# A two-layer state-space and long-convolution kernel: the list scheduler's ranks come from a table of wanted times, and A1's norm, W, G0 and the tables are computed and placed in another way

## The chip, the cores and the metric

The kernel runs on one NeuronCore of a Trainium2 chip. The metric is the device time of one execution in microseconds (us). The core has a matrix engine (PE, with its weight loads as PEld), a vector engine (DVE), a scalar engine (ACT), GpSimd (POOL) and a queue engine (SP) that issues most DMAs. Each engine executes its own instructions in the order in which the program gives them; engines wait for each other by semaphores.

## The reference

Two layer types are applied in turn, A, B, A, B, each added to a residual stream x of 2048 tokens by 640 features (bfloat16 in and out):

```python
def A(x):                      # x is already normalized, see below
    Lam_bar = exp(dt * Lam)                              # complex, 640 states
    B_bar = ((Lam_bar - 1) / Lam)[:, None] * Bmat        # 640 x 640, complex
    Bu = einsum("bld,pd->blp", x, B_bar)
    h[t] = Lam_bar * h[t-1] + Bu[:, t]                   # over 2048 tokens
    return 2 * einsum("blp,dp->bld", h, Cmat).real + x * Dskip

def B(q, k, v):                # q is the normalized x; k and v are inputs
    kv = v * (4-tap causal shift filter of k along the tokens)
    y = irfft(rfft(kv padded to 4096) * rfft(ssm_k padded))[:2048]
    return q * (y + kv * ssm_D)

x = x + A(layernorm(x)); x = x + B(layernorm(x), k, v)
x = x + A(layernorm(x)); x = x + B(layernorm(x), k, v)
```

The long convolution does not depend on x. The kernel computes it once and uses it in both B layers.

## The kernel before, in words

The program is a list of several hundred tasks, each with one engine (or a choice of ACT and DVE), dependencies, buffers and an estimate of its duration. `Sched.run` (from L121) walks through a simulated time: whenever an engine is free, it takes, among the tasks whose dependencies and buffers are there, the one with the highest rank, and the instructions are written out in the order in which tasks began. In the kernel before, a task's rank is the longest path from it to the end plus a fixed bias per part of the program:

```python
            t.path = t.est + tail + max((s.path for s in t.succ), default=0.0)
            t.rank = t.path + t.bias
```

The order of the instructions on each engine is fixed by this when the program is built.

**Phase 1, before the tokens.** The parts are: the sine tables (names `yt_*`; `FA` and `HA` are small tables that stage A and the last inverse stage need, computed on POOL with one sine on ACT each). The kv products in five blocks of 128 features: k and v are loaded transposed by SP (L907, L911), the shift filter is eight matmuls with diagonal weights for each half (L922), DVE multiplies by v (L928, the "gate"), and SP stores the block to DRAM (L932). Layer A's matrices: B is loaded and transposed by PE (L435, and with the discretization L450/451) and copied to `BT`. W0 and W1, which are C scaled by a factor per state, are made on PE as products of C (loaded transposed by SP in ten pieces, L405) with diagonal matrices `fd` that POOL builds (L343): 80 matmuls (L418/419) and 20 evacuations. G0, the direct part, is five groups (one per k) of matmuls of B with W0 (L500, L503). The rotation tables `tab` and `rtab` come from a chain of DVE, POOL and ACT instructions (L460 to L486).

Then five Y passes `yq0` to `yq4`, one per 128 features, compute the long convolution: loads of the filter and of kv, stage A (L964), stage B (L986 to L991) for the filter and for kv, the pointwise product of spectra on DVE (six instructions over 2176 elements, L1043 to L1048, called `pw`), the inverse stage IB on PE (L1067/1068), a DMA transpose by SP (`tt`, L1080), the last stage IA (L1096), and a store to DRAM (L1106). Every PE stage goes through one of four PSUM buffers, which ACT (L240) or DVE (L242) evacuates.

**Phase 2, over the tokens.** Each layer works on four chunks of 512 tokens, c0 to c3. A chunk of layer A has: layer-norm statistics (for A1 on ACT: 16 sums over the four chunks, L1236, and 16 squares, L529; for the other layers the sums come with the previous step, and ACT squares), the normalization (ACT L548 or DVE L550), a DMA transpose (`tu`, L575), 100 matmuls with BT (`bp`, L589/592), the rotation of states on DVE (`ri`, L611 to L613), two scans on DVE (L627), the rotation back (`ro`, L650 to L652), 110 or 118 matmuls with W and G (`cp`, L678), and the evacuation with the residual (`xe`, ACT L686/688 or DVE L690). A chunk of layer B is the norm, the normalization (`u`), a product with y and an addition on DVE (L714 with L716 in B1, L714 with L718 in B2, "a pair" here), and in B2 the store of the result.

## Time and profile before

| | |
|---|---|
| median of 3 runs | 424.05 us (423.93 to 424.08) |
| the profiled execution | 424.33 us |
| its span | 422.6 us |
| mean granted PE clock | 0.953 |
| PE busy | 350.3 us, 83% |
| DVE busy | 319.0 us, 75% |
| ACT busy | 251.5 us, 60% |
| POOL busy | 43.5 us, 10% |

The span goes from the first to the last instruction of one profiled execution; the rest of its time lies outside it. A row of slices divides the span into 40 equal parts of 10.6 us and shows each engine's busy share in tenths, 9 for 90% or more; PEclk is the clock granted to PE, in tenths. A row of the list of waits names an engine and a line, what it waited for, the sum in us, how often, and the longest. A row of the chain or of a timeline has the start and the duration in us, then engine and line; what stands in square brackets is the idle time ahead of it and what ended that. A row of costs has the number of instructions, then busy us and the mean of one in ns, then the idle time ahead. PE's matmuls are pipelined: one that is shown as 0.22 us long starts 0.055 us after the one before.

### The profile page before, as it was taken

How to read it: one execution, taken by the hardware profiler on the slowest of the kernel's cores; microseconds unless marked ns; L12 is line 12 of the kernel's file. 1: busy time of each engine (PE TensorE's matmuls, PEld its weight loads, DVE VectorE, ACT ScalarE, POOL GpSimd, SP SyncE). 2: the span in 40 equal slices, each digit the busy share in tenths (PEclk: the TensorE clock that was granted, in tenths of full speed). 3: DMA queues.
4: the chain of work that ended last, by engine and by line, in shares of the span. 5: the costliest groups of instructions: out<-in, count | busy, mean ns of one | idle time of the engine just before them, and what ended most of it. 6: DMA issues, size and time to landing. Idle time of an engine off the chain costs nothing.

```text
span 422.6 us, 8138 instructions
## 1 busy us (share of the span) xinstructions
PE 350.3 (83%) x3412; PEld 259.5 (61%) x3412; DVE 319.0 (75%) x430; ACT 251.5 (60%) x432; POOL 43.5 (10%) x81
## 2 busy tenths in 40 slices
PE   0596889589978898998699999999999926999920
PEld 0556758345667897897575955676887514755510
DVE  2789996301498789799999569726999995897396
ACT  1665977553899998997322764596855103402970
POOL 8727510420000000000000000000000000000000
PEclk9998999989999999999699999999999986999975
DMA  5919995944357972947721221541500300003023
GB/s 107 298 53 207 199 188 138 217 64 174 72 121 134 203 151 55 213 123 144 199 57 62 64 64 32 156 84 43 124 2 2 62 0 2 32 2 95 0 95 153
DMA packets 112542, 44.24 MB, mean 105 GB/s; under 512 B 105461, under 2 KB 106746, under 8 KB 112506
## 3 DMA queue, kind: packets, MB, share of 16 engines
q1 hardware_dynamic: 109130, 41.57, 43.8%
q10 hardware_dynamic: 3376, 2.16, 1.7%
q8 instruction: 26, 0.43, 0.4%
q14 instruction: 10, 0.08, 0.1%
HBM read 17.38 MB, written 7.86 MB: 60 GB/s over the span
## 4 chain that ended last, share of the span: by engine, by line
PE 39%; DVE 36%; ACT 10%; DMA 7%; issue 5%; POOL 2%; POOLq 0%; SPq 0%; DVEq 0%; ACTq 0%
PE ps L678 13%; DVE b L627 5%; PE ps L589 5%; PE ps L592 5%; ACT junk L529 5%; DMA b<-b 5%; DVE b L242 4%; PE ps L500 3%; DVE b L716 3%; DVE b L714 3%; PE ps L922 2%; PE ps L1067 2%; PE ps L1068 2%; DVE b L718 2%; PE ps L964 2%
## 5 line engine op out<-in xcount | busy, mean ns | idle before, releaser
L240 ACT ACTIVATE b<-ps 128x1024 bf16<-128x1024 f32 (+3 forms) x106 | 90.9, 909 | 27.5 <-PE ps L592 16.1
L678 PEld LDWEIGHTS <-b 128*128 128x128 bf16 x880 | 67.7, 98 | 48.9 <-issue 0.6
L678 PE MATMUL ps<-W,b 128*128 128x128 bf16 (+1 forms) x640 | 95.8, 299 | 0.0
L589 PE MATMUL ps<-b,BT 128*128 128x256 bf16 x400 | 59.4, 281 | 15.2 <-DVE b L690 11.6
L242 DVE CAST b<-ps 128x1024 bf16<-128x1024 f32 (+2 forms) x43 | 48.7, 1162 | 15.1 <-PE ps L1068 6.2
L592 PE MATMUL ps<-b,BT 128*128 128x256 bf16 x400 | 58.5, 278 | 0.0
L529 ACT ACTIVATE junk<-b,nmean 128x640 bf16<-128x640 f32 (+1 forms) x64 | 52.9, 827 | 1.6
L589 PEld LDWEIGHTS <-BT 128*128 128x128 bf16 x400 | 40.0, 101 | 20.9 <-issue 11.8
L627 DVE TENSOR_TENSOR_SCAN b<-rtab,b 128x1290 bf16<-128x1290 f32 x16 | 44.6, 2832 | 0.2
L592 PEld LDWEIGHTS <-BT 128*128 128x128 bf16 x400 | 40.1, 100 | 5.4
L548 ACT ACTIVATE b<-b,nmr,rstd 128x640 bf16<-128x640 f32 (+1 forms) x38 | 32.6, 911 | 15.7 <-DVE nmr L541 15.7
L524 ACT ACTIVATE nmean<-sums 128x4 f32<-128x4 f32 (+1 forms) x19 | 3.9, 203 | 59.3 <-DVE b L690 45.9
L986 PE MATMUL ps<-b,b 128*128 128x128 bf16 x170 | 35.1, 219 | 0.9 <-ACT b L240 0.6
L989 PE MATMUL ps<-b,b 128*128 128x128 bf16 x170 | 35.2, 219 | 0.0
L991 PE MATMUL ps<-b,b 128*128 128x128 bf16 x150 | 32.8, 219 | 0.0
L988 PE MATMUL ps<-b,b 128*128 128x128 bf16 x150 | 32.8, 219 | 0.0
L678 PE MATMUL ps<-G,b 128*128 128x512 bf16 (+1 forms) x160 | 27.0, 299 | 0.5 <-DVE b L690 0.5
L928 DVE TENSOR_TENSOR b<-ps,b 128x1024 bf16<-128x1024 f32 x10 | 12.1, 1222 | 18.6 <-PE ps L922 17.5
L964 PE MATMUL ps<-FA,b 128*128 128x256 bf16 x160 | 22.0, 283 | 3.1 <-ACT b L240 1.6
L539 DVE RECIPROCAL rstd<-std 128x4 f32<-128x4 f32 (+1 forms) x19 | 3.2, 168 | 24.4 <-ACT std L534 24.4
L964 PEld LDWEIGHTS <-b 128*128 128x128 bf16 x160 | 15.7, 101 | 7.2 <-issue 4.4
L1067 PE MATMUL ps<-b,b 128*128 128x128 bf16 x160 | 18.8, 219 | 1.5 <-DVE b L928 0.8
(204 smaller groups left out, 626.2 us busy)
## 6 DMA issues: line engine op xcount, KB each, us to landing
b<-in_A_x_dram SPq DMA_DIRECT2D x8, 640.0 KB, 4.2
b<-ysd SPq DMA_DIRECT2D x8, 640.0 KB, 4.4
kvd<-b SPq DMA_DIRECT2D x5, 512.0 KB
b<-kvd SPq DMA_DIRECT2D x5, 512.0 KB, 5.1
ysd<-b SPq DMA_DIRECT2D x5, 512.0 KB, 4.0
out_dram<-b SPq DMA_DIRECT2D x8, 320.0 KB, 2.3
b<-in_B_ssm_k_dram SPq DMA_DIRECT2D x4, 512.0 KB
b<-in_A_B_re_dram ACTq DMA_DIRECT2D x1, 800.0 KB
```

The source lines that it names most:

```text
L240: nc.scalar.activation(out, in_, ACT.Copy)
L242: nc.vector.tensor_copy(out, in_)
L529: nc.scalar.activation(small.junk, src(q), ACT.Square, bias=st["nmean"][:, i:i + 1], scale=1.0, accum_out=st["ssq"][:, i:i + 1])
L589: nc.tensor.matmul(pb[:, jj, c2, :], lhsT=aw["BT1"][:, c2, j, k, :], rhs=uT[:, k, 0:2, :].rearrange("p t i -> p (t i)"), start=(k == 0), s ...
L592: nc.tensor.matmul(pb[:, jj, c2, :], lhsT=aw["BT0"][:, c2, k, j * P:(j + 1) * P], rhs=uT[:, k, 2:4, :].rearrange("p t i -> p (t i)"), star ...
L627: nc.vector.tensor_tensor_scan(gv, rt, gv, 0.0, ALU.mult, ALU.add)
L678: nc.tensor.matmul(pc[:, o0:o1], lhsT=lh, rhs=rh, start=(n == 0), stop=(n == len(ops) - 1))
L964: nc.tensor.matmul(pa[:, o4, :], lhsT=s_x.get()[:, 4 * g + o4, :], rhs=T["FA"][:], start=True, stop=True)
L986: nc.tensor.matmul(ps[:, g, 0, :], lhsT=T["Cf"].get()[:, q, :], rhs=are, start=True, stop=single)
L988: nc.tensor.matmul(ps[:, g, 0, :], lhsT=T["Sf"].get()[:, q, :], rhs=A[:, 2 * q + 1, :], start=False, stop=True)
L989: nc.tensor.matmul(ps[:, g, 1, :], lhsT=T["NSf"].get()[:, q, :], rhs=are, start=True, stop=single)
L991: nc.tensor.matmul(ps[:, g, 1, :], lhsT=T["Cf"].get()[:, q, :], rhs=A[:, 2 * q + 1, :], start=False, stop=True)
```

## The change

1. **Order.** A table `WHEN` gives a number to each group of tasks (the name up to a colon; some 270 groups), and the rank becomes minus this number plus a thousandth of the path. Some estimates of durations and latencies are other numbers too. So the order of the instructions is another one on all engines.
2. **W.** W0 and W1 are made by ACT (one C part scaled by a factor per partition into a float buffer) and DVE (`scalar_tensor_tensor`: the other part times its factor plus that buffer), 20 instructions each over 640 elements. The 80 matmuls, the POOL diagonals and the 20 evacuations go. C is loaded for W0 and again for W1: 20 DMA transposes of 128 x 640 instead of ten.
3. **B and G0.** B is loaded in ten pieces by ACT's queue directly into the tiles in which G0 and `tab` will stand later, so two large buffers are free. G0's matmuls need W0 (not W1) and stand ahead of the tables; the tables wait for all of G0's matmuls.
4. **Norm of A1.** `bn_stats` on DVE (two instructions of 320 columns and one `bn_aggr` per 128 tokens) in place of ACT's sums and squares.
5. **FA and HA.** POOL makes only the index ramps; the arithmetic is on DVE, the sine on ACT.
6. The small parameter vectors are loaded by ACT's queue instead of SP's.

The diff, cut to its core:

```diff
+WHEN = {
+    "yt_io0": -271.6, "yt_ph0": 326, "yt_sin0": -120, "yt_neg0": -228.7, "yt_io6": 435.5, "yt_ph6": 22.8, "yt_sin6": -279.2, "yt_neg6": -141, "yt_io12":
...
+}
-            t.rank = t.path + t.bias
+            t.rank = t.path + t.bias if WHEN is None else 0.001 * t.path - WHEN.get(t.name.partition(":")[0], 0)
...
-            nc.scalar.dma_start(out=s_B[i].get(), in_=src.rearrange("(j p) e -> p j e", p=P))
+            for k in range(NJ):
+                nc.scalar.dma_start(out=B[i][:, k], in_=src[:, k * P:(k + 1) * P].rearrange("(j p) e -> p j e", p=P))
...
-                    for d0, d1 in ((0, 512), (512, D)):
-                        nc.tensor.matmul(pw[:, d0:d1], lhsT=fd[:, 3 * w + c, :], rhs=wr[:, 0, d0:d1], start=True, stop=False)
-                        nc.tensor.matmul(pw[:, d0:d1], lhsT=fd[:, 3 * w + c + 1, :], rhs=wr[:, 1, d0:d1], start=False, stop=True)
...
+                def e_wc(_, w=w, c=c, j=j, s_wr=s_wr):
+                    nc.scalar.activation(s_wr.get()[1], s_wr.get()[0][:, 1, :], ACT.Copy, scale=st["F6"][:, w, c + 1, j:j + 1])
+                def e_wm(_, w=w, c=c, j=j, s_wr=s_wr):
+                    nc.vector.scalar_tensor_tensor(aw["W1" if w else "W0"][:, c, j, :], s_wr.get()[0][:, 0, :], st["F6"][:, w, c, j:j + 1], s_wr.get()[1],
+                                                   ALU.mult, ALU.add)
...
-        t_m = S.add(f"a_gm{k}", "pe", 10 * c_mm(512) + 11 * c_mm(P), [t_dd] + ws + T["tab"], e_gm, uses=[s_pg] + s_B)
+        t_m = S.add(f"a_gm{k}", "pe", 10 * c_mm(512) + 11 * c_mm(P), [t_dd] + w0s + bms, e_gm, uses=[s_pg])
...
-    t_t0 = S.add("a_t0", "dve", 5.7, [t_p4], e_t0)
+    t_t0 = S.add("a_t0", "dve", 8.3, gms, e_t0, uses=[s_tt])
...
+            for h in range(2):
+                nc.vector.bn_stats(bs[:, h, :], src(q)[:, h * (D // 2):(h + 1) * (D // 2)])
+            nc.vector.bn_aggr(st["mv"][:, q, :], bs[:])
...
-                nc.scalar.activation(small.junk, s_xb.get()[:, q, :], ACT.Copy, accum_out=su(0, c)[:, q:q + 1])
```

The table's numbers tell a reader little; what it does to the order is seen from the rows of the two programs. Three places follow. A row has the line in the program's source, the operation, and output and inputs; in the changed kernel the lines are some 75 higher (L242 is L289 there, L500 is L512, L714 and L718 are L788 and L792, L690 is L764, L928 is L1006, L1043 to L1048 are L1121 to L1126).

The first is PE in phase 1, at the end of the W matmuls in the kernel before, which are followed by the first of G0's five groups (`fd` is the diagonal, `b_0_95` is B):

```order
L418 MATMUL ps_104<-b_3_85,fd_101 128x128
L419 LDWEIGHTS fd_101
L419 MATMUL ps_104<-b_3_85,fd_101 128x128
L500 LDWEIGHTS b_0_95
L500 MATMUL ps_106<-W_112,b_0_95 128x512
L500 LDWEIGHTS b_0_95
```

And PE in the changed kernel at the end of G0's first group, where B lies in the tiles `G` and `tab`:

```order
L512 MATMUL ps_106<-W_112,tab 128x128
L512 LDWEIGHTS tab
L512 MATMUL ps_106<-W_112,tab 128x128
L1042 LDWEIGHTS b_1_83
L1042 MATMUL ps_105<-FA,b_1_83 128x256
L1042 LDWEIGHTS b_1_83
```

In the kernel before, the five groups of G0 (105 matmuls) stand one behind the other after the last W matmul. In the changed kernel there are no W matmuls, and each of the five groups stands alone between stages of the Y passes; the first is followed by stage A (L1042) of a pass.

The second is DVE between the pointwise product of pass 0 and that of pass 1. In the kernel before, the rows from the last two kv gates to the product's first instruction are these (`G_114` is G0):

```order
L928 TENSOR_TENSOR b_3_85<-ps_106,b_3_85 128x1024
L1013 TENSOR_TENSOR b_0_82<-b_0_82,kd 128x16
L928 TENSOR_TENSOR b_1_83<-ps_103,b_1_83 128x1024
L928 TENSOR_TENSOR b_1_83<-ps_105,b_1_83 128x1024
L242 CAST G_114<-ps_104 128x640
L242 CAST b_1_96<-ps_105 128x1024
L242 CAST b_1_96<-ps_103 128x1024
L242 CAST b_1_96<-ps_104 128x1024
L1043 TENSOR_TENSOR b_3_98<-b_1_96,b_2_97 128x2176
```

In the changed kernel the same stretch ends so (L462 is the W step):

```order
L1006 TENSOR_TENSOR b_2_84<-ps_103,b_2_84 128x1024
L462 SCALAR_TENSOR_TENSOR W_112<-b_7_89,s_F_434 128x640
L462 SCALAR_TENSOR_TENSOR W_112<-b_0_82,s_F_434 128x640
L289 CAST b_5_100<-ps_103 128x8x32x4
L289 CAST b_5_100<-ps_105 128x2x32x4
L462 SCALAR_TENSOR_TENSOR W_112<-b_7_89,s_F_434 128x640
L289 CAST b_3_98<-ps_104 128x1024
L462 SCALAR_TENSOR_TENSOR W_112<-b_0_82,s_F_434 128x640
L1091 TENSOR_TENSOR b_8_90<-b_8_90,kd 128x16
L289 CAST b_0_95<-ps_103 128x4x32x8
L289 CAST b_1_96<-ps_106 128x1024
L1121 TENSOR_TENSOR b_0_95<-b_1_96,b_3_98 128x2176
```

Six of the ten kv gates and one of G0's evacuations stand between the two products before; two gates, four W steps and no evacuation of G0 stand there now, and the gates of the last two kv blocks come behind the second product.

The third is the end of DVE's work. In the kernel before, the last twelve rows are these (`b_6_88` and `b_1_83` are the results of chunks c2 and c3):

```order
L714 TENSOR_TENSOR b_5_87<-b_5_87,b_6_88 128x640
L718 TENSOR_TENSOR b_6_88<-b_5_87,b_5_100 128x640
L714 TENSOR_TENSOR b_5_87<-b_5_87,b_6_88 128x640
L718 TENSOR_TENSOR b_6_88<-b_5_87,b_5_100 128x640
L714 TENSOR_TENSOR b_0_82<-b_0_82,b_1_83 128x640
L718 TENSOR_TENSOR b_1_83<-b_0_82,b_0_95 128x640
L714 TENSOR_TENSOR b_0_82<-b_0_82,b_1_83 128x640
L718 TENSOR_TENSOR b_1_83<-b_0_82,b_0_95 128x640
L714 TENSOR_TENSOR b_0_82<-b_0_82,b_1_83 128x640
L718 TENSOR_TENSOR b_1_83<-b_0_82,b_0_95 128x640
L714 TENSOR_TENSOR b_0_82<-b_0_82,b_1_83 128x640
L718 TENSOR_TENSOR b_1_83<-b_0_82,b_0_95 128x640
```

In the changed kernel the last residual evacuation (L764) and all that follows it but the last three rows, which are of the same kind, are these:

```order
L764 SCALAR_TENSOR_TENSOR b_3_98,sums_4420<-ps_105,b_3_98 128x640
L584 RECIPROCAL rstd_1_4525<-std_1_4522 128x1
L586 TENSOR_TENSOR nmr_1_4527<-nmean_5_4517,rstd_1_4525 128x1
L788 TENSOR_TENSOR b_3_85<-b_3_85,b_9_91 128x640
L792 TENSOR_TENSOR b_9_91<-b_3_85,b_3_98 128x640
L788 TENSOR_TENSOR b_3_85<-b_3_85,b_9_91 128x640
L792 TENSOR_TENSOR b_9_91<-b_3_85,b_3_98 128x640
L584 RECIPROCAL rstd_2_4540<-std_2_4535 128x1
L586 TENSOR_TENSOR nmr_2_4542<-nmean_6_4529,rstd_2_4540 128x1
L788 TENSOR_TENSOR b_3_85<-b_3_85,b_9_91 128x640
```

Eleven pairs stand behind the last residual evacuation before; four stand there now, and those of chunks c1 and c2 are ahead of it.

More of the change, by code (lines that the diff above doesn't have):

```diff
@@ L428, in a_setup_tasks @@
+    bts, bms = [], []
     for c in range(2):
@@ L457, in a_setup_tasks, with e_gm, e_ge @@
     T["bt"] = bts
+    gs, gms = [], []
+    for k in range(NJ):
+        s_pg = R_ps.new()
+        def e_gm(_, k=k, s_pg=s_pg):
+            pg = s_pg.get()
+            ksl = slice(k * P, (k + 1) * P)
+            for d0, d1 in ((0, 512), (512, D)):
+                here = d0 <= k * P < d1
+                for c in range(2):
+                    for j in range(NJ):
+                        nc.tensor.matmul(pg[:, d0:d1], lhsT=B[c][:, k, j, :], rhs=aw["W0"][:, c, j, d0:d1], start=(c == 0 and j == 0),
+                                         stop=(c == 1 and j == NJ - 1 and not here))
+                if here:
+                    nc.tensor.matmul(pg[:, ksl], lhsT=ident[:], rhs=aw["DD"][:, k, :], start=False, stop=True)
+        t_m = S.add(f"a_gm{k}", "pe", 10 * c_mm(512) + 11 * c_mm(P), [t_dd] + w0s + bms, e_gm, uses=[s_pg])
+        gms.append(t_m)
+        def e_ge(eng, k=k, s_pg=s_pg):
+            evac(nc, eng, aw["G0"][:, k, :], s_pg.get()[:, 0:D])
+        gs.append(S.add(f"a_ge{k}", ("act", "dve"), (c_act(D), c_tt(D, True)), [t_m], e_ge, uses=[s_pg]))
@@ new lines, in y_table_tasks, with e_f3, e_f4 @@
+    t_f2 = S.add("yt_f2", "dve", 2.6, [t_f0, t_f1], e_f2, bias=5, uses=[s_fa])
+    def e_f3(_):
+        for a, n in ((768, 256), (1088, 64)):
+            nc.scalar.activation(part(a, n), part(a, n), ACT.Sin, scale=TWO_PI / 32.0)
+    t_f3 = S.add("yt_f3", "act", 0.55, [t_f2], e_f3, bias=5, uses=[s_fa])
+    def e_f4(_):
+        nc.vector.tensor_tensor(T["FA"][:], part(768, 256), part(512, 256), ALU.mult)
+        nc.vector.tensor_tensor(T["HA"][:], part(1088, 64), part(1152, 64), ALU.mult)
```

294 lines of the change are left out of this document (139 added, 155 removed), and 45 rows, old and new, of the table WHEN.

## The prediction, made before the changed kernel ran

> **What bounds the kernel now.** The page comes first: it says whether one engine is the limit everywhere, or whether the limit changes along the span.
>
> ```profile
> span 422.6 us, 8138 instructions
> PE 350.3 (83%) x3412; PEld 259.5 (61%) x3412; DVE 319.0 (75%) x430; ACT 251.5 (60%) x432; POOL 43.5 (10%) x81
> PE   0596889589978898998699999999999926999920
> DVE  2789996301498789799999569726999995897396
> PEclk9998999989999999999699999999999986999975
> DMA  5919995944357972947721221541500300003023
> PE 39%; DVE 36%; ACT 10%; DMA 7%; issue 5%; POOL 2%; POOLq 0%; SPq 0%; DVEq 0%; ACTq 0%
> ```
>
> No engine is the limit over the whole span. In the chain that ended last, PE has 39% and DVE 36%, in turns. Three places stand out in the slices: DVE drops to 3, 0 and 1 at about 74 to 105 us, PE drops to 2 at about 342 to 352, and PE ends at 2 and 0 while DVE is still at 9. The windows give the first and the last of them in numbers (after the length of the window: PE, PEld, DVE, ACT).
>
> ```profile
> 80.00:100.00 20.00, 15.63 (x87) 7.81 (x86) 2.77 (x3) 10.13 (x16) 4.42 (x4) 0.91 0.51 115
> 100.00:120.00 20.00, 17.06 (x206) 12.17 (x204) 7.78 (x7) 14.45 (x30) 0.00 (x0) 1.00 0.49 126
> 120.00:140.00 20.00, 17.73 (x287) 16.28 (x285) 17.94 (x20) 19.73 (x28) 0.00 (x0) 1.00 0.75 141
> 220.00:240.00 20.00, 20.00 (x175) 14.29 (x174) 15.22 (x17) 8.91 (x20) 0.00 (x0) 1.00 0.22 67
> 400.00:423.00 23.00, 3.66 (x37) 2.30 (x34) 18.56 (x37) 9.17 (x17) 0.00 (x0) 0.65 0.31 114
> ```
>
> From 80 to 120 us DVE has 10.55 us of work in 40; from 120 on DVE and ACT are both nearly full, and from 220 on PE is. The list of waits names what it waits for, and the chain and the DVE timeline show what is between two passes.
>
> ```profile
> DVE b L928 <- PE ps L922: 17.5, 5, 13.7
> DVE G L242 <- PE ps L500: 11.0, 1, 11.0
> PE ps L589 <- DVE b L690: 11.6, 1, 11.6
> ```
> ```profile
> 20.96 2.67 PE ps L964 x12
> 97.90 2.16 PE ps L500 x10
> 100.11 2.72 PE ps L500 x20
> 108.43 3.07 PE ps L500 x27
> 111.50 6.73 DMA b<-b
> 155.08 1.29 DVE b L1043
> 403.70 0.83 DVE b L690 x2
> 418.63 0.82 DVE b L718
> ```
> ```profile
> 61.19 1.29 DVE L1048 TENSOR_TENSOR b<-b,b 128x2176 bf16<-128x2176 bf16 x1
> 116.49 1.29 DVE L1043 TENSOR_TENSOR b<-b,b 128x2176 bf16<-128x2176 bf16 x1 [0.25 <-ACT b L240]
> 136.48 1.29 DVE L1043 TENSOR_TENSOR b<-b,b 128x2176 bf16<-128x2176 bf16 x1
> 161.47 1.29 DVE L1048 TENSOR_TENSOR b<-b,b 128x2176 bf16<-128x2176 bf16 x1
> 203.19 1.48 DVE L611 TENSOR_TENSOR b<-b,tab 128x2560 bf16<-128x2560 bf16 x1
> ...
> 298.66 1.49 DVE L611 TENSOR_TENSOR b<-b,tab 128x2560 bf16<-128x2560 bf16 x1 [0.59 <-ACT b L240]
> ...
> 384.26 1.50 DVE L652 TENSOR_TENSOR b<-b 128x2580 bf16<-128x2580 bf16 x1
> ```
>
> The pointwise product of Y pass 0 ends at 62.5 and that of pass 1 starts at 116.5, 54 us later. The next two starts follow at 20.0 and 18.6 us. So one gap holds some 34 us too much: the last kv gates wait 13.7 us behind PE's W matmuls, then PE runs G0 (L500) from 97.9 to 111.5 in one piece, and pass 0's transpose and pass 1's inputs come only then. At the end, 15 us pass between the last residual evacuation (403.7) and the last output addition.
>
> **The change, part by part.** The time is summed as a walk along the order of the changed kernel, with the durations of this profile.
>
> *W without PE.* 80 matmuls go, as 40 pairs of 512 and 128 columns. The row L500 x20 is ten such pairs in 2.72 us, so PE loses 40 x 0.272 = 10.9 us, all of it between the passes. In their place ACT and DVE get 20 instructions each; ACT's 20 evacuations of W go.
>
> ```profile
> L240 ACT ACTIVATE W<-ps 128x640 bf16<-128x640 f32 x20 | 13.1, 705 | 11.0 <-PE ps L419 11.0
> L718 DVE TENSOR_TENSOR b<-b,b 128x640 bf16<-128x640 bf16 x16 | 13.2, 825 | 0.6
> L714 DVE TENSOR_TENSOR b<-b,b 128x640 bf16<-128x640 bf16 x32 | 15.5, 485 | 0.0
> L1236 ACT ACTIVATE junk<-b 128x640 bf16<-128x640 bf16 x16 | 11.8, 734 | 0.8 <-DMA b<-in_A_x_dram 0.5
> L529 ACT ACTIVATE junk<-b,nmean 128x640 bf16<-128x640 bf16 x16 | 13.2, 826 | 0.3
> L534 ACT ACT_TABLE_LOAD x1 | 1.3, 1283 | 0.0
> ```
>
> ACT comes out even (20 x 0.70 for 20 x 0.705). DVE gains 20 x 0.825 = 16.5 us; the bounds are 9.7 (at 0.485) and 16.5, and I take the upper since one input is f32. Most of it falls into the gap where DVE was idle; what is left in the later gaps is counted below.
>
> *Norm by bn_stats.* ACT loses 16 x (0.734 + 0.826) = 25 us beside the accumulator reads. DVE gets 32 instructions over 320 elements and 16 small ones. The trace has no such instruction. Half an L714 is 0.24, half an L718 is 0.41, a whole L718 0.825; so 32 of them cost 8 to 26 us. I take 0.42, the half of the row that reads at one element a cycle, and 0.16 to 0.25 for each small one: 16 us. Chunks 0 to 2 (12 us) stand before the fifth product and are counted there; chunk 3's lies where PE is the limit.
>
> *A second price for ACT.* ACT loads an activation table six times instead of four: 2 x 1.283 = 2.6 us in the first phase, where ACT is nearly as full as DVE. The Trainium skill ("ScalarE: Activation LUTs", What ACT_TABLE_LOAD costs) adds a drain of about 1.38 us to each switch and so speaks a little against the change; by it the two would be 5.3 us and the time 3 us later. The row shows only the load.
>
> *The first steps start later.*
>
> ```profile
> 11.65 5.47 SPq L907 DMA_TRANSPOSE b<-in_B_k_dram  x1
> ```
>
> B's loads are ten transfers on ACT's queue ahead of ACT's first sine, two of them waiting for the K transposes, whose second ends at 17.1; FA goes from POOL to DVE and ACT and is ready about when the sines end. The first stage A (20.96 above) moves to about 30. Other work fills part of it; I count the end of pass 0's product at 66 instead of 62.5 (bounds 62 and 71: nothing lost, all 9 lost).
>
> *Pass to pass.* W no longer stands in front of pass 0's inverse transform, and G0's five groups are single, each between stages of the passes. What DVE has between two products is, by its rows: 6 evacuations or gates of 1.2 and 4 W steps (11 us, 14 with ACT's share) before pass 1; 16 us before pass 2; 16 us with the norm of chunk 0 and 1, against ACT's 21, before pass 3. A product is 6 x 1.28 = 7.7. So 66 + 14 + 7.7 + 18 + 7.7 + 22 + 7.7 = 143 for the end of the third (before: 162.8).
>
> *A1 ahead of pass 4.* Now DVE has 18.5 us of W, tables and norm, A1 chunk 0's rotation, scan and rotation back (17 us), and then the fifth product, 7.7: 143 + 18.5 + 17 + 7.7 = 186 to 188 for A1 chunk 1's rotation, which is at 203.19 before. Gain so far 15 us.
>
> *PE's stretch.* From there PE is the limit, as it is before. By the pitch of its matmuls (0.272 for a pair as above, 0.055 for 128 columns, 0.11 for 256), the order has 66 us of PE work from pass 4's inverse (done at 192) to the last bp matmul of A2's chunk 0: 258 to 260. Its rotation starts at 262, before at 298.66: 37 us less. Counted another way: PE's work ahead of that point falls from 235 to 216 us, by the 10.9 of W and by part of A1's last cp, which is put behind it; the other 18 are idle time, 63 before, 44 now. PE has 104 us left at 260.
>
> *DVE's stretch.* From A2 chunk 0's rotation to the end of chunk 3's, DVE has four times 15.5 us and the residual work between: 82 us by rows, 87 in the trace of before (298.66 to 385.76). 262 + 86 = 348. PE's remaining 104 us would end at 364.
>
> *The tail.* After 348, DVE has 18 us of evacuations and pairs up to the last evacuation; PE's end, at 364 with it, is close to that: 368. Before, eleven pairs of 0.485 + 0.825 stand behind it, now four. From the last evacuation's end (404.5) to the end of the span is 18.1 us. Four pairs, four small instructions and the same 3 us of store make 5.9 + 3.1 = 9. I allow one more microsecond because the norm of the last rows comes through ACT. 368 + 10 = 378.
>
> The profiled execution takes 424.33 us, its span 422.6: 1.7 outside it. The median of the three runs is 424.05, 0.3 less. 378 + 1.7 = **380 us**, 44 less, of which 37 are there when A2 starts and 8 to 9 come from the shorter tail. What is cancelled: PE's wait of 11.6 (L589 for L690, in which PE waits for the end of chunk 2's residual) should go since that order is changed too; DVE's total rises by 3 to 7 us.
>
> **The rivals.**
>
> *Half of it is eaten by waits in order.* Each of PE's groups now waits for a PSUM buffer which the engine behind it has to empty, with four buffers for all. For it: DVE and ACT are both over 16 us in 20 from 120 on, and my gaps hold work only with no wait between engines. Against: the waits between passes (12 and 11 us gaps before) are part of the gaps already. With 5 us lost in each of the four passes, 380 + 20 = 400.
>
> *The early loads are the limit.* SP issues twenty transposes of C instead of ten.
>
> ```profile
> 82.08 1.26 SPq L405 DMA_TRANSPOSE b<-in_A_C_im_dram  x1
> 129.86 4.86 SPq L1080 DMA_TRANSPOSE b<-b  x1
> ```
>
> Ten more take 10 x 1.26 = 12.6 us on a queue that issues in order, and the DMA slices from 21 to 63 us are at 9, 9, 9, 5, 9, 4. If they all come before the loads that a pass waits for: 392. The Trainium skill ("DMA: Bandwidth & Descriptors", Rules for kernel authors) says that DMAs from different issuing engines run on the same 16 DMA engines; so loads moved from SP to ACT would give nothing here. No run yet shows it.
>
> *Slower: SP's order chains the passes.*
>
> ```profile
> b<-kvd SPq DMA_DIRECT2D x5, 512.0 KB, 5.1
> ```
>
> SP stores pass q's result ahead of loading pass q+2's V, and the store waits for the whole inverse. If each pass needs transpose 4.9, its landing 1.8 (6.73 in all above), inverse and evacuation 4, load 5.1, forward evacuations 9, product 7.7, inverse 6 one after the other, a pass takes 39 us and the fifth product ends at 66 + 4 x 39 = 222 instead of 188: 414. With 3 us per pass for the C transposes between, it is 426, slower. It decides if V of pass q+1 is loaded only after pass q's store. The order shows V of the next pass one place ahead for passes 1 and 3, so I give it little.
>
> *It does not reach phase 2.* The passes end early, but A2 chunk 0 starts no more than 15 us earlier, since PE is full from 220 on: 424 - 15 - 11 (tail and PE's wait) = 398. This is near the first rival.
>
> **How the numbers follow.** Forecast 0.48; waits or phase 2 at 398 to 400: 0.30; loads at 392: 0.12; slower 0.05; still faster than all of it, by cheap bn_stats and a start without loss (380 - 8 - 4 = 368): 0.05. Two in ten may be left out: the range goes from 366, just under that last case, to 404, past the first rival and the upper bn price (380 + 10). A measurement of this kernel tells apart about 0.2%, 0.85 us. Faster 0.94, same 0.01, slower 0.05.
>
> **What would show it.** In the changed profile: the start of the second product at about 80 and of A1 chunk 1's rotation near 188; no PE group of L512 longer than one k in a row; a bn_stats near 0.42; A2 chunk 0's rotation near 262; less than 10 us from the last residual evacuation to the end. The forecast is wrong if A2's first rotation stays beyond 280, if PE's idle time between 260 and 360 exceeds 15 us, or if SP's V loads wait for stores.

## The result, and the profile after

The changed kernel takes 370.71 us (median of 4 runs, 369.93 to 371.3) against 424.06 us for the kernel before (4 runs, 423.93 to 424.87): a ratio of 0.874, with a 95% interval of 0.872 to 0.876, 53 us less. The prediction was 380 with a range of 366 to 404. The profiled execution takes 369.93 us; its span is 368.1.

Its page, the lines that answer to those of before:

```profile
span 368.1 us, 7994 instructions
PE 329.2 (89%) x3332; PEld 247.8 (67%) x3332; DVE 316.3 (86%) x483; ACT 258.2 (70%) x402; POOL 22.1 (6%) x54
PE   0259998999998899899999999999999999999990
DVE  8666579699699799399998999977978999999996
PEclk9999999999999999999999999999999999999996
PE 70%; ACT 13%; DVE 9%; issue 3%; DMA 2%; POOL 1%; ACTq 1%; DVEq 0%; POOLq 0%
```

The three holes are gone: DVE's 3, 0 and 1 in the first third, PE's 2 near the end, and the tail in which only DVE worked. DVE's total is almost what it was (319.0 before); PE's is 21 us less: the W matmuls are 10.9 of it, and the granted clock probably has part in the rest (its mean was 0.953 and is 0.992; seven slices of PEclk stood below 9, now only the last). So what was removed is mostly idle time: 368.1 - 316.3 = 52 us on DVE, where it was 103.6. The last line is the chain that ended last: PE has 70% of it and DVE 9%. The experiments on A2 below show that this does not make PE the limit there. The windows give the same places as before, and the last 28 us (after the length: PE, PEld, DVE, ACT):

```profile
80.00:100.00 20.00, 19.74 (x222) 14.95 (x220) 16.59 (x18) 15.87 (x20) 0.00 (x0) 1.00 1.06 225
100.00:120.00 20.00, 18.79 (x255) 15.17 (x253) 19.63 (x35) 17.94 (x23) 0.00 (x0) 1.00 1.05 205
360.00:368.00 8.00, 0.00 (x0) 0.00 (x0) 4.76 (x10) 2.56 (x5) 0.00 (x0) 0.62 0.21 83
```

From 80 to 120 us DVE works 36 of 40 us instead of 10.6, and after 360 only the 8 us of the last pairs are left. DVE's timeline has the milestones on which the prediction walked (L1121 and L1126 are the first and the last instruction of a pointwise product, L685 the first of a rotation of A, L726 the last of the last rotation back, L764 the last residual evacuation, whose row is the chain's):

```profile
58.68 2.02 DVE L1126 TENSOR_TENSOR b<-b,b 128x2176 bf16<-128x2176 bf16 x1
75.28 1.29 DVE L1121 TENSOR_TENSOR b<-b,b 128x2176 bf16<-128x2176 bf16 x1
102.29 1.28 DVE L1121 TENSOR_TENSOR b<-b,b 128x2176 bf16<-128x2176 bf16 x1
126.62 1.28 DVE L1121 TENSOR_TENSOR b<-b,b 128x2176 bf16<-128x2176 bf16 x1
132.99 1.29 DVE L1126 TENSOR_TENSOR b<-b,b 128x2176 bf16<-128x2176 bf16 x1
158.03 1.49 DVE L685 TENSOR_TENSOR b<-b,tab 128x2560 bf16<-128x2560 bf16 x1
182.26 1.49 DVE L685 TENSOR_TENSOR b<-b,tab 128x2560 bf16<-128x2560 bf16 x1
255.59 1.49 DVE L685 TENSOR_TENSOR b<-b,tab 128x2560 bf16<-128x2560 bf16 x1
340.37 1.50 DVE L726 TENSOR_TENSOR b<-b 128x2580 bf16<-128x2580 bf16 x1
358.51 0.83 DVE b L764 x2
```

Step by step, in us, with the prediction's own terms (a term is the time from the milestone above it):

| up to | predicted | measured |
|---|---|---|
| end of the first product | 66 | 60.7 |
| end of the fourth (gaps 14, 18, 22 predicted; 14.6, 19.3, 16.7 measured) | 77 | 73.6 |
| first rotation of A1 | 18.5 | 23.7 |
| A1 chunk c1's rotation | 25 | 24.2 |
| A2 chunk c0's rotation | 75.5 | 73.3 |
| end of chunk c3's rotation back | 86 | 86.3 |
| end of the last residual evacuation | 20 | 17.5 |
| end of the span | 10 | 8.8 |
| sum | 378 | 368.1 |

Half of the 10 us by which the sum was too high is the start. The third row went the other way, by 5.2 us: had it been right, the sum would have been 15 us too high, so that the forecast came this near is in part luck.

### The profile page after: what moved, and what is told of

Read it like the earlier page. It is cut to its first block, busy times and chain, and to the rows that moved or that the text cites. A ratio compares the mean times of both kernels' runs of the same rounds, so it can differ in the third digit from the quotient of the medians.

```text
span 368.1 us, 7994 instructions
## 1 busy us (share of the span) xinstructions
PE 329.2 (89%) x3332; PEld 247.8 (67%) x3332; DVE 316.3 (86%) x483; ACT 258.2 (70%) x402; POOL 22.1 (6%) x54
## 4 chain that ended last, share of the span: by engine, by line
PE 70%; ACT 13%; DVE 9%; issue 3%; DMA 2%; POOL 1%; ACTq 1%; DVEq 0%; POOLq 0%
PE ps L752 32%; PE ps L663 10%; PE ps L666 10%; ACT b L287 8%; PE ps L1000 5%; PE ps L512 3%; PE ps L1042 2%; DMA b<-in_B_ssm_k_dram 2%; DVE bs L599 2%; PE ps L1145 1%; PE ps L1146 1%; PE ps L1064 1%; ACT b L458 1%; PE ps L1067 1%; POOL b L392 1%
## 5 line engine op out<-in xcount | busy, mean ns | idle before, releaser
L287 ACT ACTIVATE b<-ps 128x1024 bf16<-128x1024 f32 (+3 forms) x126 | 110.2, 956 | 17.4 <-PE ps L666 14.8
L663 PE MATMUL ps<-b,BT 128*128 128x256 bf16 x400 | 56.7, 273 | 0.6 <-ACT b L287 0.5
L666 PE MATMUL ps<-b,BT 128*128 128x256 bf16 x400 | 56.7, 273 | 0.0
L619 ACT ACTIVATE b<-b,nmr,rstd 128x640 bf16<-128x640 f32 (+1 forms) x51 | 44.0, 918 | 7.4 <-DVE nmr L586 7.3
L663 PEld LDWEIGHTS <-BT 128*128 128x128 bf16 x400 | 38.7, 98 | 5.2 <-issue 0.9
L666 PEld LDWEIGHTS <-BT 128*128 128x128 bf16 x400 | 39.1, 98 | 4.5
L574 ACT ACTIVATE junk<-b,nmean 128x640 bf16<-128x640 f32 x48 | 39.8, 828 | 1.5
L289 DVE CAST b<-ps 128x1024 bf16<-128x1024 f32 (+1 forms) x23 | 23.5, 1045 | 13.1 <-PE ps L1069 7.1
L760 ACT ACTIVATE b<-ps 128x640 f32<-128x640 f32 x16 | 11.2, 699 | 21.6 <-PE ps L752 21.5
L1042 PE MATMUL ps<-FA,b 128*128 128x256 bf16 x160 | 22.6, 285 | 3.3 <-ACT b L287 1.8
L569 ACT ACTIVATE nmean<-sums 128x4 f32<-128x4 f32 (+1 forms) x15 | 3.0, 203 | 29.0 <-DVE b L764 22.7
L1042 PEld LDWEIGHTS <-b 128*128 128x128 bf16 x160 | 15.8, 102 | 7.9 <-issue 3.9
L1000 PE MATMUL ps<-b,fd 128*128 128x512 bf16 x80 | 18.4, 379 | 0.6 <-ACT b L287 0.6
```

Of the source, the lines that this page charges most:

```text
L287: nc.scalar.activation(out, in_, ACT.Copy)
L574: nc.scalar.activation(small.junk, src(q), ACT.Square, bias=st["nmean"][:, i:i + 1], scale=1.0, accum_out=st["ssq"][:, i:i + 1])
L619: nc.scalar.activation(dst, src, ACT.Identity, bias=st["nmr"][:, i:i + 1], scale=st["rstd"][:, i:i + 1])
L663: nc.tensor.matmul(pb[:, jj, c2, :], lhsT=aw["BT1"][:, c2, j, k, :], rhs=uT[:, k, 0:2, :].rearrange("p t i -> p (t i)"), start=(k == 0), s ...
L666: nc.tensor.matmul(pb[:, jj, c2, :], lhsT=aw["BT0"][:, c2, k, j * P:(j + 1) * P], rhs=uT[:, k, 2:4, :].rearrange("p t i -> p (t i)"), star ...
L1000: nc.tensor.matmul(pk[:, 512 * b:512 * (b + 1)], lhsT=s_ds.get()[:, l, :], rhs=kT[:, t0:t0 + 512], start=(l == 0), stop=(l == 3))
```

## The experiments

They came in two kinds. The first four take the changed kernel and put one of its parts back as it was, and leave it to the list scheduler, with its table of wanted times, to write out the order anew.

**The order alone.** The changed kernel with all its parts, but with the old ranks:

```diff
+WHEN = None
```

> The changed kernel with the old rank (longest path plus bias) in place of the table; W, the norm, B, FA and HA stay as changed. Theory 'order': the parts alone spare PE 10.9 us and move work between ACT and DVE, but most of the 53 us come from the order of the tasks; G0 is a block again and nine pairs of additions stand behind the last evacuation: 398 to 412 us. Rival 'parts': what was moved off PE and ACT brings the gain, the order only a little: below 382 us.

It takes 424.35 us (10 runs), above both ranges; the ratio to before is 0.999 (0.995 to 1.002). Under the old ranks the parts bring nothing, so the gain needs the new order. Whether it also needs the parts is another question: the old parts under an order as good as this one were not run. A2's first rotation stands where it stood in the kernel before (298.66 there):

```profile
299.79 1.49 DVE L688 TENSOR_TENSOR b<-b,tab 128x2560 bf16<-128x2560 bf16 x1 [4.65 <-ACT b L290]
```

**W by PE again**, in the place and with the wanted times of the new W steps:

```diff
-    nc.scalar.activation(s_wr.get()[1], s_wr.get()[0][:, 1, :], ACT.Copy, scale=...)
-    nc.vector.scalar_tensor_tensor(aw["W1" if w else "W0"][:, c, j, :], ...)
+    nc.tensor.matmul(pw[:, d0:d1], lhsT=fd[:, 3 * w + c, :], rhs=wr[:, 0, d0:d1], start=True, stop=False)
+    nc.tensor.matmul(pw[:, d0:d1], lhsT=fd[:, 3 * w + c + 1, :], rhs=wr[:, 1, d0:d1], start=False, stop=True)
```

> The changed kernel with W made again by 80 PE matmuls, diagonals and evacuations (C loaded once), the table kept. Theory 'PE is the limit from its first matmul on': 10.9 us of PE work come back and the time rises by as much, 381 to 383 us. Rival 'they fit into PE's idle time': PE has some 45 us without work before 159 us, and DVE loses 17 us there, so the time is 368 to 374 us.

411.11 us; ratio 0.967 (0.960 to 0.973). Both theories missed.

**A1's norm by ACT again**, in the wanted times of the new one:

```diff
+for c_ in range(4):
+    for n_ in (f"xs{c_}", f"A1c{c_}_ln_nm", f"A1c{c_}_ln_sq"):
+        WHEN[n_] = WHEN[f"A1c{c_}_ln_bn"]
```

> The changed kernel with A1's norm by sums and squares on ACT again, the table kept. Theory 'ACT limits the passes': ACT has 19.88 of 20 us busy at 140 to 160; with 31 us more there and 17 less on DVE the stretch of gapless PE begins 5 to 12 us later: 376 to 383 us. Rival 'DVE limits the passes': 16 us less on DVE make it faster: 363 to 369 us.

417.55 us; ratio 0.983 (0.978 to 0.988). Both missed.

**G0's five groups with the highest rank**, so that they stand together:

```diff
+for k_ in range(5):
+    WHEN[f"a_gm{k_}"] = -3000 + k_
```

> The changed kernel with G0's five groups one behind the other on PE (rank highest), as before the change, all else as changed. Theory 'a block of 13.6 us on PE holds up the next pass': A1's first rotation and the end come 5 to 10 us later, 376 to 381 us. Rival 'PE's total decides': nothing is added to PE, the passes have slack for it: 369 to 373 us.

428.25 us (10 runs); ratio 1.008 (1.005 to 1.011). Both missed: the kernel is 0.8% slower than the one before the change.

The last three misses have one reason. The table fits exactly one list of tasks. With 80 more matmuls, or with five other ranks, the scheduler's simulated time runs differently, and the rest of the program is placed differently too. With W on PE, A2's first rotation is at 267.33 in DVE's timeline, 11.7 later than in the changed kernel. That this is near W's 10.9 means little, since A1's first rotation is 26.2 later (184.25). From A2's first rotation to that of chunk c3 (371.17) it takes 103.8 us, where the changed kernel takes 69.3 (255.59 to 324.92). Those 34 us in a phase that has nothing to do with W are the order. With the norm on ACT the same stretch takes 102.5 us, with G0's ranks 106.3. So these three runs say nothing on what a part is worth.

The other experiments therefore freeze the order: the changed kernel's own order of all tasks is taken as it came out, named tasks are moved within it, and nothing else is planned anew. (`place(order, names, anchor)` puts the tasks behind the anchor.) All else stays in its order. Their lines are some 45 higher than the changed kernel's.

**G0 in one piece.** The groups move together with their evacuations (`a_ge`).

```diff
+    return place(order, ["a_gm4", "a_ge0", "a_gm2", "a_ge4", "a_gm1", "a_ge2", "a_gm3", "a_ge1", "a_ge3"], "a_gm0")
```

> The changed kernel with the order of all its instructions kept as it is, except that G0's five groups stand one behind the other on PE, where its first group stands. Theory that the single groups matter (G0 in one piece, 105 matmuls of some 11 to 13.5 us, holds back the stages of the next pass): the product behind it starts 4 to 10 us later, and the time rises by 3 to 8 us, to 374 to 379. Rival, that PE's total decides in phase 1: the same matmuls, 0 (370 to 372).

383.9 us; ratio 0.902 (0.898 to 0.906), 13 us more than the changed kernel: the theory in kind, and twice its size. The windows show a hole again, smaller than that of the kernel before: DVE has 10.29 us of work in 20 (it was 10.55 in 40).

```profile
100.00:120.00 20.00, 17.62 (x231) 13.79 (x231) 10.29 (x10) 14.06 (x17) 0.00 (x0) 1.00 0.99 184
120.00:140.00 20.00, 13.76 (x163) 12.15 (x163) 16.41 (x38) 15.86 (x20) 0.00 (x0) 0.91 0.53 107
140.00:160.00 20.00, 17.22 (x191) 16.01 (x191) 17.67 (x24) 18.11 (x24) 0.37 (x1) 0.83 0.48 106
```

```profile
115.14 1.28 DVE L1165 TENSOR_TENSOR b<-b,b 128x2176 bf16<-128x2176 bf16 x1
140.24 1.28 DVE L1165 TENSOR_TENSOR b<-b,b 128x2176 bf16<-128x2176 bf16 x1
188.59 1.28 DVE L1165 TENSOR_TENSOR b<-b,b 128x2176 bf16<-128x2176 bf16 x1
```

The third product starts 39.0 us after the second (at 76.12), where it was 27.0: 12.0 us more for four groups, some 11 us, that now stand ahead of it. What surprises is that the four groups that were taken out from between the later passes give nothing back: the next two products follow at 25.1 and 48.4 us, against 24.3 and 48.1. Part of that may be the clock, which the windows show at 0.91 and 0.83 from 120 to 160 us (1.00 in the changed kernel); it wasn't separated from the other engines' work there.

**G0's matmuls twice,** each group where it stands, so that only PE has more to do, in pieces:

```diff
-            for d0, d1 in ((0, 512), (512, D)):
+            for d0, d1 in ((0, 512), (512, D)) * 2:
```

> The changed kernel with its order kept; each of G0's five groups of matmuls is executed twice, so PE has some 13.5 us more in phase 1, at five places of 2.7 us between the stages of the passes; this is about what the W matmuls (10.9 us) would bring, spread. Theory that PE's time there stands on the path between the passes, as the prediction counted W's 10.9 us: +9 to +13 (380 to 384). Rival, that PE's idle time of phase 1 takes it up when it comes in small pieces: 0 to +4 (371 to 375).

383.93 us; ratio 0.904 (0.901 to 0.908): 13.2 us for some 13.6 us of PE work. The third instructions of the five products, in DVE's timeline:

```profile
56.40 1.29 DVE L1170 TENSOR_TENSOR b<-b 128x2176 bf16<-128x2176 bf16 x1
79.38 1.29 DVE L1170 TENSOR_TENSOR b<-b 128x2176 bf16<-128x2176 bf16 x1
109.15 1.29 DVE L1170 TENSOR_TENSOR b<-b 128x2176 bf16<-128x2176 bf16 x1
140.36 1.29 DVE L1170 TENSOR_TENSOR b<-b 128x2176 bf16<-128x2176 bf16 x1
193.56 1.29 DVE L1170 TENSOR_TENSOR b<-b 128x2176 bf16<-128x2176 bf16 x1
```

Their distances are 22.98, 29.77, 31.21 and 53.20 us; in the changed kernel 22.98, 27.01, 24.32 and 48.06. So the four gaps grow by 0, 2.8, 6.9 and 5.1 us, and no, one, two and two of the added groups fall into them. That is 14.8 us in this execution, whose span is 16.4 longer; the other 1.6 lie ahead of the first product, where nothing was changed. Five groups of 2.7 us are 13.6: they land whole on the path, although PE is idle for 0.3 to 2.4 us in every 20 from 80 to 160 us in the changed kernel. None of that idle time took anything up. Extra PE work between the passes costs what it takes, as the prediction took W's 10.9 us. (In the third gap it costs more, 6.9 for two groups; the windows show the clock at 0.91 from 120 to 140 us there, which may have part in it.)

**Half of bn_stats left out.**

```diff
-            for h in range(2):
+            for h in range(1):
                 nc.vector.bn_stats(bs[:, h, :], src(q)[:, h * (D // 2):(h + 1) * (D // 2)])
-            nc.vector.bn_aggr(st["mv"][:, q, :], bs[:])
+            nc.vector.bn_aggr(st["mv"][:, q, :], bs[:, 0:1, :])
```

> The changed kernel with its order kept; A1's statistics are taken from the first 320 of the 640 features only, so 16 of the 32 bn_stats go (16 x 0.415 = 6.6 us of DVE; 5.0 of them, chunks 0 to 2, stand before A1's first rotation). Theory that DVE's norm stands on the path as the prediction counted it (12 us before the fifth product): -3 to -5 us (366 to 368). Rival, that it lies in DVE's waits before 159 us (DVE busy 14.2 of 20 there): 0 to -1.

370.6 us; ratio 0.872 (0.869 to 0.874): nothing. The statistics of two chunks stand between the third and the fourth product. With half of them gone the fourth still starts 24.32 us after the third (24.33 in the changed kernel). DVE waits for ACT's root instead, 3.54 us where it was 0.33, and ACT is busy for 16.6 of the 16.6 us between the two products in both kernels.

```profile
122.50 0.18 DVE L654 RECIPROCAL rstd<-std 128x4 f32<-128x4 f32 x1 [3.54 <-ACT std L649]
```

The statistics of the third chunk stand behind the fourth product. From its first instruction to A1's first rotation it is 159.43 - 128.03 = 31.40 us here and 158.03 - 126.62 = 31.41 in the changed kernel. The windows of that stretch, the changed kernel first, then this one:

```profile
134.00:159.00 25.00, 22.65 (x291) 20.41 (x289) 18.47 (x37) 24.14 (x30) 0.00 (x0) 1.00 0.53 99
```
```profile
135.50:160.50 25.00, 22.66 (x291) 20.51 (x290) 17.00 (x33) 24.14 (x30) 0.00 (x0) 1.00 0.53 100
```

DVE has 6.5 us to spare and gets 1.5 more, so it is not the limit there. ACT works 24.14 of 25 us in both, and the changed kernel's chain runs through ACT from 135.7 to 159 us with short gaps. That points to ACT, but no run changed ACT's work there, and PE is close: G0's two doubled groups near the start of this stretch cost 5.1 of their 5.5 us (above). ACT's groups in that stretch of the changed kernel:

```profile
L287 ACT ACTIVATE b<-ps 128x1024 bf16<-128x1024 f32 (+3 forms) x15 | 12.6, 911 | 0.0
L619 ACT ACTIVATE b<-b,nmr,rstd 128x640 bf16<-128x640 bf16 x4 | 3.5, 967 | 0.0
L458 ACT ACTIVATE b<-b,s_F 128x640 f32<-128x640 bf16 x3 | 2.5, 849 | 0.0
L541 ACT ACTIVATE tab<-rtab,half_pi 128x1290 bf16<-128x1290 f32 x1 | 1.4, 1370 | 0.0
L539 ACT ACT_TABLE_LOAD x1 | 1.3, 1283 | 0.0
L605 ACT ACT_TABLE_LOAD x1 | 1.3, 1283 | 0.0
```

Evacuations are half of it. The change put 9 us there: three W steps (2.5 us), the three instructions that make the rotation tables (L539 to L541, 3.9 us), and two table loads (2.6 us), one for the sine of these tables and one back to the norm's root (L605). In the kernel before, ACT made the rotation tables at 46.1 to 50.0 us, while its sine table was still loaded; now they wait for all of G0 and fall behind the first root, at 120.8.

**Less work for PE in A2.**

```diff
-                        for k in range(NJ):
+                        for k in range(NJ - 1 if (self.lname, c) == ("A2", 1) else 0, NJ):
                             nc.tensor.matmul(pb[:, jj, c2, :], lhsT=aw["BT0"][:, c2, k, j * P:(j + 1) * P], ...)
```

> The changed kernel with its order kept; 40 of the 100 bp matmuls of A2's chunk c1 are left out, so its states lack part of their input. At a pitch of 0.109 us PE has 4.4 us less, in the stretch that shows no gap on PE. Theory that PE's work bounds the time from 160 us on: -4 to -4.5 (366). Rival, DVE with 19.6 of 20 us is as near: -1 to -2, since DVE's work then holds the end.

370.75 us; ratio 0.872 (0.869 to 0.875): nothing, less than either theory said.

**More work for DVE in A2.**

```diff
-            for c2 in range(2):
-                gv = g[:, c2].rearrange("p j b -> p (j b)")
+            for c2 in range(4 if (self.lname, c) == ("A2", 1) else 2):
+                gv = g[:, c2 % 2].rearrange("p j b -> p (j b)")
```

> The changed kernel with its order kept; the two scans of A2's chunk c1 are executed twice, so DVE has some 5.6 us more in the stretch where it shows 19.5 of 20 us. Theory that PE alone bounds it: 0 to +3. Theory that DVE is as near as PE from A2's chunk c0 on, as the prediction's walk over DVE's 86 us took: +4.5 to +6 (375 to 377).

375.18 us; ratio 0.883 (0.880 to 0.887): 4.5 us of the 5.5. The two runs are read together. First the start of chunk c2's rotation, in the kernel with less PE work and in the one with more DVE work, and then, from their pages, PE's bp group and what it waited for:

```profile
300.70 1.49 DVE L729 TENSOR_TENSOR b<-b,tab 128x2560 bf16<-128x2560 bf16 x1
```
```profile
305.27 1.49 DVE L729 TENSOR_TENSOR b<-b,tab 128x2560 bf16<-128x2560 bf16 x1
```
```profile
L707 PE MATMUL ps<-b,BT 128*128 128x256 bf16 x400 | 57.3, 276 | 2.8 <-DVE b L808 2.2
```
```profile
L707 PE MATMUL ps<-b,BT 128*128 128x256 bf16 x400 | 57.7, 276 | 3.9 <-DVE b L808 3.3
```

The matmuls left out stand between the rotations of c0 and c1. These are 27.39 us apart without them (256.33 and 283.72) and 27.35 in the changed kernel. The rotation of chunk c1 starts at 283.72 in the one and at 282.81 in the other, so from c1 to c2 it is 16.98 and 22.46 us; the changed kernel has 16.99 (282.94 to 299.93). Work taken from PE moved nothing, and 2.2 of its 4.4 us came back as a wait for DVE's residual evacuation (L808), which the changed kernel does not have; work given to DVE went through whole at that place, and 5.0 us of it is left at the last evacuation. From c1 on DVE sets the pace, although the changed kernel's trace shows PE with 20.00 of 20 us busy in every window from 280 to 340 and DVE with 19.3 to 19.6. From c0 to c1 it is not DVE's work alone: DVE is busy for 16.4 of 20 us from 260 to 280 and waits 3.3 us at 276.8 for a root from ACT. PE is so near that any more DVE work shows up as idle time on it.

**The tail.** Chunk c2's four pairs and their store go back behind the last residual evacuation:

```diff
+    return place(order, ["B2c2_m", "B2c2_st"], "A2c3_xe")
```

> The changed kernel with its order kept, except that the four pairs and the store of B2's chunk c2 stand behind the last residual evacuation: eight pairs after it instead of four. Theory of the tail (what DVE has behind the last evacuation is the end): 4 pairs of 1.27 us, +5.1 us, 375 to 377. Rival (the norm of the last chunk, which goes through ACT, sets the end and DVE waits there): 0 to +2.

375.69 us; ratio 0.884 (0.881 to 0.887), 5.0 us more: four pairs of 1.27. In the chain the pairs follow each other up to the store with only the small instructions of the norm between them, in the changed kernel too; the norm of the last rows, through ACT, is hidden behind them.

**The start.** The first of two: B's loads behind the last sine, what the first pass needs ahead of the other table, and B's transposes with their evacuations (`seq`, `es`) later.

```diff
...
+    order = place(order, seq + es[-1:], "kv_mm1:0")
+    order = place(order, ["a_ldB1", "a_ldB0"], "yt_sin12")
+    order = place(order, ["kv_dsl"], "a_pl")
+    order = place(order, ["a_p0", "kv_d0", "yt_neg0", "yt_f3", "yt_f4", "yq0_ka"], "yt_ph12", after=False)
+    order = place(order, ["kv_d1", "kv_d2", "kv_ds0"], "a_p1")
```

> The changed kernel with its order kept, except at the start: B's ten loads stand behind the last table sine on ACT's queue, FA's arithmetic and the first loads' consumers stand ahead of the other table's, and B's transposes and their evacuations come behind the second group of the kv filter. The first stage A should start at 13 to 15 us instead of 23.2. Theory that the start of the first pass carries through to the end (as 61 instead of the 66 that the prediction took did): 361 to 366. Rival, that B's later transposes and loads hold the matrices or G0, or that kv's loads arrive no sooner: 369 to 372.

383.88 us; ratio 0.903 (0.901 to 0.906), 13 us more, which neither theory had. Stage A did start at 17.64 instead of 23.21. But then ACT's timeline, the chain, and DVE's timeline say:

```profile
20.03 8.31 ACTq L496 DMA_DIRECT2D G<-in_A_B_re_dram  x5
28.37 1.28 ACT L417 ACT_TABLE_LOAD   x1 [10.04 <-DMA G<-in_A_B_re_dram]
```
```profile
18.35 8.44 DMA b<-b
26.81 0.38 ACTq L496
```
```profile
65.69 1.29 DVE L1175 TENSOR_TENSOR b<-b,b 128x2176 bf16<-128x2176 bf16 x1
```

The third of the second five loads is issued only at 26.81, when a DMA transpose of the sines has landed (18.35, 8.44 us long), and ACT, whose queue issues it, does nothing for 10 us. Why this load waits for that transfer the trace does not say; a semaphore that both use in turn would explain it, and is not shown. Stage A's evacuations stand behind it. The first product starts at 65.69 instead of 52.30, 13.4 later, and the span is 381.5 instead of 368.1, 13.4 longer. A delay of the start goes through to the end whole.

**The start, the second.** Only the first sines come ahead of the loads, and the two groups of five are apart:

```diff
+    order = place(order, ["yt_f3", "kv_dsl", "a_ldB1"], "yt_sin0")
+    order = place(order, ["a_ldB0"], "a_p3")
+    order = place(order, ["yt_neg0", "yt_f4", "kv_d0", "yq0_ka"], "a_p0")
```

> The changed kernel with its order kept, except at the start: on ACT's queue the first sines come ahead of all of B's loads, whose first five stand behind FA's sine (at about 11 us) and whose last five stand behind the small exponential that follows the last sine (at about 18 us), so that neither group should have to wait long for an earlier transfer; on DVE the arithmetic of FA and of the first filter comes ahead of what waits for B. The sines should end at 17 to 18 us instead of 22.3, the first stage A start at 19 to 20 instead of 23.2. Theory that ACT's queue, held by the loads' issues, set the start, and that the start carries through one to one: -3 to -5 us (366 to 368). Rival, that the transfers themselves (the DMA engines busy in nine tenths from 2 to 26 us) set it, so that B or the transposed sines only land later: 0 to +3 (371 to 374).

369.74 us (5 runs); ratio 0.869 (0.866 to 0.871). The span is 367.9, 0.2 shorter, and the first product starts at 52.02, 0.3 earlier. Single traces cannot tell that apart: the first product starts anywhere from 52.20 to 53.87 in the traces of the six runs whose edits lie behind it. Between sets of runs the ratio of kernels with the same path (the two above that changed nothing) varies as much. So it is one us at best, and neither range has it. Of the 3 to 5 us expected, the sines brought 3.2 (they end at 19.1 instead of 22.3), and the first four matmuls of stage A start at 19.30 instead of 23.21, as expected. In the chain it is seen how they went:

```profile
11.74 4.18 DMA tab<-in_A_B_im_dram
20.69 1.26 ACTq L489
22.00 0.71 ACT BT L334
26.07 4.89 PE ps L1047 x16
31.11 1.05 POOL fd L1024
```

Two waits of the loads' issues are still on the chain, before the sines and before the first evacuation (22.00 instead of 23.73, 1.7 us left). And the 16 filter matmuls take 4.89 us, where the changed kernel's take 3.47 (27.77 to 31.24), which leaves 0.3. The theory is half right: the queue held the sines and stage A, but what is behind them was hardly earlier.

## Why the prediction was right, point by point

- **What bounds it; the order.** Right: the gap between two passes, PE's hole at 342 and the tail are what went. With the old ranks nothing is gained, so there is no gain without the order; what of it needs the new parts stays open. G0 in one piece brings a hole back and costs 13 us.
- **W without PE.** 10.9 us between the passes: likely right in size. G0's matmuls, added there in W's stead, cost what they take (13.2 for 13.6); W's own were not put back with the order kept. DVE's 20 steps take 17.4 us (the first row below) where 16.5 was taken from L718.
- **Norm by bn_stats.** The price was right: 13.5 us for the 32 instructions (the second row) and 3.3 for the 16 small ones, 16.8 together, where 16 were taken. That 12 us of it count before the fifth product was wrong: 8 of them lie in the gap that the prediction itself took by ACT's 21 us, the other 4 in its 18.5, and with half of them gone neither stretch moved.

```profile
L462 DVE SCALAR_TENSOR_TENSOR W<-b,s_F 128x640 bf16<-128x640 bf16 x20 | 17.4, 873 | 1.1 <-ACT b L458 1.0
L599 DVE BATCH_NORM_STATS2 bs<-b 128x6 f32<-128x320 bf16 x32 | 13.5, 462 | 0.0
```

- **A1 ahead of pass 4.** The step that failed. It counted DVE's 18.5 us. DVE has 17.2 us of work there, but the stretch took 23.7, and DVE's work is not what sets it: less of it changed nothing. ACT is busy for 22.9 of the 23.7 us and PE for 21.9; that ACT is the limit is likely and not shown. The prediction's remark that the two more table loads come in a phase "where ACT is nearly as full as DVE" points at it: both lie in that stretch (at 146.3 and 153.4), and so do ACT's 3.9 us for the rotation tables, but none of them was put into the sum. A load is 1.283 us and the next instruction follows at once (for the one at 22.32: 22.32 + 1.28 = 23.60, the next begins at 23.61), so no run here shows the drain that the Trainium skill ("ScalarE: Activation LUTs", What ACT_TABLE_LOAD costs) states.
- **The start.** The term that was mis-sized: 66 taken, 60.7 measured, below even the lower bound of 62. Stage A begins at 23.21, not near 30: B's loads held ACT's queue to 12.9 and the first sine to 15.5, not to 17 and later. That is not all of it: from stage A's start to the product's end it is 37.5 us where the kernel before has 41.5 (20.96 to 62.48), a gain for which the prediction had no term, and which part of the change made it is open. The price of every us there is one us at the end, which the first start experiment showed from the other side.
- **Pass to pass.** 54 for the three gaps, 50.6 measured; the third was taken too long (22, by ACT's 21; ACT has 16.6 there and is never idle), the other two together 2 us too short.
- **PE's stretch, 183 to 256.** 75.5 taken, 73.3 measured. That PE is the limit there was not tested. It has 20.00 of 20 us in the windows, but so it has from 256 on, where it isn't the limit; this stays open.
- **DVE's stretch.** 86 taken, 86.3 measured. The two experiments on A2 show that PE does not set it, and from chunk c1 on that DVE does; between c0 and c1 the wait for ACT's root has part in it. The prediction carried PE's end at 364 beside it as nearly equal; PE's last matmuls end at 358.5, and the last evacuation waits 0.19 us for them.
- **The tail.** 10 taken, 8.8 measured; four pairs more cost 5.0. The microsecond for the norm through ACT was not needed.
- **The rivals.** Waits in order, loads as the limit, a chain through SP's stores, and an early end of phase 1 that doesn't reach phase 2: none came in the size that was forecast. One load, a filter's, stands on the changed kernel's chain (6.91 us at 103.53); in the run with half of bn_stats the chain goes through ACT there and the distances are the same. A1's c1, A2's c0 and the end follow the passes at the forecast distances, and in the experiments delays of 13 us between the passes reached the end whole.

## What to carry to other kernels

In a program whose engines run in a fixed order, a hole is found where one engine waits in front of a long run of another's work that could have stood elsewhere; what filling it is worth is the walk along the order, stage by stage, with the engine that is fullest in each stage, and ACT is to be counted there like the others. A table of times that steers a list scheduler belongs to one exact list of tasks: to price one part of such a change, freeze the order and move or double single tasks, since here each edit that was left to the scheduler made a new schedule. "Busy all the time" does not name the limit: take work from one engine and give work to the other, and see which moves the end.

## What the runs showed of the hardware

**Loads on a computing engine's queue.** The five loads of B_im take 7.14 us of ACT's queue in the changed kernel, although each issue alone takes only 0.37 to 0.54: the second starts at 9.57, and what it waits for is not shown. The first sine starts at 15.5 (in the second start experiment, where no load of B stands ahead of it, at 6.9):

```profile
5.73 7.14 ACTq L442 DMA_DIRECT2D tab<-in_A_B_im_dram  x5
14.24 1.28 ACT L845 ACT_TABLE_LOAD   x1 [14.24 <-DVE b L837]
```

The row names DVE as what ended the wait; but DVE has the first sine's input ready at 6.85 in both kernels, and in the experiment the sine starts right then, so here it was the queue. The Trainium skill ("DMA: Bandwidth & Descriptors", Rules for kernel authors) says that spreading DMAs over the issuing engines "only saves sequencer issue time". Here it cost such time, on an engine that had other work.

**Matmuls at half speed at the start.** In the second start experiment the filter matmuls of 512 columns, and those of the changed kernel a little later (timeline; a row's duration is one latency, 0.63 and 0.38, and a pitch for each further matmul):

```profile
25.87 1.49 PE L1047 MATMUL ps<-b,fd 128*128 128x512 bf16 x3
```
```profile
28.69 1.46 PE L1000 MATMUL ps<-b,fd 128*128 128x512 bf16 x6
```

The pitch is (1.49 - 0.63) / 2 = 0.43 us in the one and (1.46 - 0.38) / 5 = 0.216 in the other, while the windows show a granted clock of 1.00 in both. The Trainium skill ("TensorE: Matmul & The Clock Gate", What's actually happening) says that what is issued in the first 3.4 us or so of activity runs at half the clock; by that, matmuls that are moved ahead, while PE is still mostly idle, run slower. The rows agree on the half speed but not on its length: PE's dense work begins at 22.8 there and the slow pitch lasts to about 28.8, some 6 us (16 matmuls in 4.89 us are six or seven at 0.43 and the rest at 0.216). A window's granted clock does not show it.
